# Chunk 0 of a sketched attention by halves of its tokens, with the remaining keys and one sketch load moved

## The chip, the cores and the metric

The kernel runs on one core of a Trainium2 chip. Its time is the device time of one execution in microseconds (us); smaller is better. The engines are PE (TensorE, with PEld for its weight loads), DVE (VectorE), ACT (ScalarE), POOL (GpSimd) and SP (SyncE, which here only issues DMAs). Each engine works through its own instructions in the order of the program text: the kernel ties every instruction to the one before it on its engine.

## The reference

Attention with sketched features, whose result goes into a two-layer perceptron with an exact gelu:

```python
batch, n_heads, seq, head_dim = (4, 4, 1088, 32)   # r = 8
def phi(x):
    a = np.einsum('rd,bhsd->bhsr', S1, x)
    b = np.einsum('rd,bhsd->bhsr', S2, x)
    return np.einsum('bhsi,bhsj->bhsij', a, b).reshape(*x.shape[:-1], r * r)
q_p, k_p = (phi(q), phi(k))
kv = np.einsum('bhsf,bhsd->bhfd', k_p, v)
z = np.sum(k_p, axis=2)
num = np.einsum('bhsf,bhfd->bhsd', q_p, kv)
den = np.einsum('bhsf,bhf->bhs', q_p, z)[..., None] + 1e-06
x = (num / den)              # to (4352, 128): tokens by heads * head_dim
h = x @ w_in                 # 128 -> 2048
g = 0.5 * h * (1.0 + erf(h * inv_sqrt2))
out = g @ w_out              # 2048 -> 128
```

S1, S2, w_in and w_out come as float64; q, k and v as float32.

## The kernel before, in words

**Tokens.** Each of the four batches has 1088 tokens: 1024 in two chunks of 512, and 64 that remain. So there are eight chunks (n = 0 to 7) and one last chunk of the remaining tokens of all batches. For each chunk the 2048 hidden features are 16 tiles `fi` of 128: `hidden(n, fi)` is one product of 128x128 by 128x512 on PE (two passes of 0.43 us each in fp32) into a bank `h_ps`, of which there are two, and a gelu on ACT from it, which frees the bank. `project` and `two_products` multiply the gelus by w_out.

**Prologue.** Before this stream runs, batch 0 needs its attention. The names:
- `sketches` turns the sketch S (S1 above S2) on PE (L319). S itself arrives as float64 words in `raw_SR` (L177) and is rounded to float32 by `Rounding` into `SR_heads`.
- `key_turn` transposes keys on PE (L333), `key_features` multiplies them by the sketches (L375) and forms the features `k_p` on DVE or POOL.
- `key_turn_rem` and `key_features_rem` do so for the 64 remaining keys of batches 0 and 2 (L333, L399, then L404 and L405).
- `kv_first` and `kv_first_rem` sum features by values into `kv_bank` (L432, L438), with the sums z as extra columns; the result is copied to `kz[0]` by ACT (L794).
- `query_turn(n)` transposes queries: chunk 1 on PE (L333, then a copy `qT` by ACT), the others on DVE. `expand_products(n)` (L497) expands them on PE into two double banks `w_ps`; `expand_copy` copies one factor out on ACT to `A_sb` (L504), `expand_multiply` makes `q_pT` on DVE (L510).
- `attend_by_token(n)`, for chunks 0 and 1, multiplies `q_pT` by `kz` (L562, tokens on the partitions), adds 1e-6 to the denominators (L567), inverts them (L568) and multiplies (L570) into `x_tok`; `turn_x` transposes that on PE (L578) and copies it to `xT` on ACT and DVE (L581), which `hidden` reads.

**Weights.** Every piece of w_in and w_out arrives as float64 words and is rounded by `Rounding` in steps: `low_words` and `exponents` on ACT (L267, L279), `fields`, `mantissas` and `signs` on DVE (L271, L273, L287, L292), and `product` on DVE or POOL (L297). The first two pieces of each have 256 columns.

**Loads.** Nearly all are issued by SP in the order of the text. `load_w_out(i, gated=True)` first lets POOL write one element of the landing tile (L168), so that SP can't issue the load before POOL has come there; everything SP issues later stands behind it.

**Order.** Until step 4 the order is written out by hand; then `steps` gives the order of `hidden(n, fi)`, first features 0 to 3 of chunk 0, then those of chunk 1, and so on, with slots between them. `keep_busy` issues a product of noughts whose result nobody reads. Lines whose order the change touches:

```python
    query_turn(1, lambda **a: late.append(a))
    act.copy(out=kz[0], in_=kv_bank[:, :128])
    ...
    banks = [hidden_bank(), hidden_bank()]
    attend_by_token(0, banks)
    expand_products(1)
    w_in[1].mantissas()
    expand_copy(1, 0)
    turn_x(0, [hidden_bank(), hidden_bank()])
    keep_busy(1, out_bank())
```

Of the kernel before, what the change touches and what calls it, by code (L numbers as in the profile page):

```python
# [16 lines left out]
def kernel(  # L17
# [49 lines left out]
    def work_banks():  # L67

        return wps.tile([128, 2, CW], FP, name="w_ps")
# [93 lines left out]
    def load_w_out(i, gated=False):  # L163
        src, e = words(moe_w_out)
        to = landing(w_out_sb[i], e == 2)
        if gated:

            pool.memset(to[0:1, 0:1], 0)  # L168
        sp.dma_start(
            out=to.rearrange("p (fo d) -> p fo d", d=d_model * e),  # L170
            in_=src[slice(*pieces[i]), :].rearrange("(fo fi) d -> fi fo d", fi=128))

    S_dst = landing(SR, S1.dtype != FP)

    for i, s in enumerate((S1, S2)):
        s, e = words(s)
        act.dma_start(out=S_dst[i * R:(i + 1) * R, :], in_=s)  # L177
    nc.scalar.preload_act_table_set("gelu_and_others")
    for r in range(2):
        load_main(sp, "k", 0, slice(r, H, 2))  # L180
# [217 lines left out]
    def key_features_rem(pair, ps, by_pool=False):  # L398
        pe.matmul(ps[:, 384:448], lhsT=kT["rem"][:, :128], rhs=S12.rearrange("p h r -> p (h r)"), start=True, stop=True)  # L399
        k_p_rem[pair] = big.tile([128, H, R, R], FP, name=f"k_p_rem{pair}")  # L400
        ab = ps[:, 384:448].rearrange("p (h r) -> p h r", r=2 * R)
        both = att.tile([128, H, 2 * R], FP, name="a_rem")
        if by_pool:
            act.copy(out=both, in_=ab)  # L404
            pool.tensor_mul(**spread(k_p_rem[pair], both[:, :, 0:R], both[:, :, R:2 * R]))  # L405
            return
        a = both[:, :, 0:R]
        act.copy(out=a, in_=ab[:, :, 0:R])
        dve.tensor_mul(**spread(k_p_rem[pair], a, ab[:, :, R:2 * R]))
# [16 lines left out]
    def kv_first(ps, r, tokens=range(J)):  # L426

        for i in tokens:

            ch, t, one = i // 4, i // 2 % 2, i % 2  # L430
            for c in range(NP):
                pe.matmul(ps[c * F:(c + 1) * F, r * 2 * D:(r + 1) * 2 * D], lhsT=flat(k_p[0, r][:, t, c * 4 + ch * 2 + one]),  # L432
                          rhs=v_aug[r][:, c, i, :], start=(r == 0 and i == 0), stop=False, skip_group_check=True)
# [68 lines left out]
    def expand_copy(n, i):  # L502
        A[i] = att.tile([128, 2, CW // 2], FP, name="A_sb")
        act.copy(out=A[i][:, :, :width[n] // 2], in_=B_of[n][i][:, :, :width[n] // 2])  # L504
# [44 lines left out]

    x_tok = {}  # L550

    def attend_by_token(n, banks, meanwhile=lambda: None):

        x_tok[n] = att.tile([128, JC, H, D], FP, name="x_tok", bufs=1)
        den = att.tile([128, NP, JC * 2], FP, name="den_tok")
        for i in range(JC):
            for r in range(2):
                for half in range(2):
                    for c in range(NP):
                        rows, at, tok = slice(c * F, (c + 1) * F), (i * 2 + r) * C, i * 128 + half * 64  # L560
                        v_at = kz_cols(0, 2 * c + r)[0]
                        pe.matmul(banks[c][half * 64:(half + 1) * 64, at:at + C], lhsT=qp[n][rows, r, tok:tok + 64],  # L562
                                  rhs=kz[0][rows, v_at:v_at + C], start=True, stop=True)
        meanwhile()
        nd = [banks[c][:, :JC * 2 * C].rearrange("p (g c) -> p g c", c=C) for c in range(NP)]
        for c in range(NP):
            dve.tensor_scalar(out=den[:, c], in0=nd[c][:, :, D], scalar1=1e-6, scalar2=None, op0=AX.add)  # L567
        dve.reciprocal(out=den, in_=den)  # L568
        for c in range(NP):
            dve.tensor_mul(out=x_tok[n][:, :, 2 * c:2 * c + 2], in0=nd[c][:, :, 0:D].rearrange("p (j r) d -> p j r d", r=2),  # L570
                           in1=den[:, c].rearrange("p (j r) -> p j r", r=2)[:, :, :, None].broadcast_to([128, JC, 2, D]))

    def turn_x(n, banks):

        xT[n] = att.tile([128, CW], FP, name="xT", bufs=3)
        for i, ps in enumerate(banks):
            for j in range(2):
                pe.transpose(ps[:, j * 128:(j + 1) * 128], in_=x_tok[n][:, 2 * i + j].rearrange("p h d -> p (h d)"),  # L578
                             identity=ident)
        for i, (ps, copy) in enumerate(zip(banks, (by_act, by_dve))):  # L580
            copy(out=xT[n][:, i * 256:(i + 1) * 256], in_=ps[:, :256])  # L581


    g_of, o_of = {}, {}
# [1 line left out]
    def w_tile(w, fi):  # L586
        i = max(i for i, (c0, c1) in enumerate(pieces) if c0 <= fi * 128)
        at = fi * 128 - CUTS[i]
        return w[i][:, at:at + 128]

    def hidden(n, fi, by_halves=False):
        W = width[n]
        ps = hidden_bank()
        w = w_tile(w_in_sb, fi)
        for rows in (slice(0, 64), slice(64, 128)) if by_halves else (slice(0, 128),):
            pe.matmul(ps[rows, :W], lhsT=w[:, rows], rhs=xT[n][:, :W], start=True, stop=True)  # L596
        if n < NCH and fi < USUAL:
            g_of[n, fi] = mlp.tile([128, CW], FP, name="g", bufs=4)
        else:
            if fi % NB == 0:  # L600
                blocks[n, fi // NB] = block(FP)
            g_of[n, fi] = blocks[n, fi // NB][:, fi % NB]
        act.activation(out=g_of[n, fi][:, :W], in_=ps[:, :W], func=ACT.Gelu)  # L603

# [172 lines left out]
    for i in range(2):  # L777
        query_features(0, i)
    kv_bank = out_bank()
    kv_first(kv_bank, 0)  # L780
    key_turn_rem(0, banks[1], by_act)
    kv_first(kv_bank, 1, range(J // 2))
    key_features_rem(0, banks[1], by_pool=True)
    load_w_out(0, gated=True)
    kv_first(kv_bank, 1, range(J // 2, J))
    kv_first_rem(kv_bank)
    w_in = [Rounding(w) for w in w_in_sb[:2]]
    w_out = [Rounding(w_out_sb[0], beside=w_in[0])]
    w_in[0].low_words()
    w_in[0].fields()  # L790
    w_in[0].exponents()
    late = []
    query_turn(1, lambda **a: late.append(a))
    act.copy(out=kz[0], in_=kv_bank[:, :128])  # L794
    w_in[1].low_words()
    by_act(**late[0])
    w_in[0].mantissas()
    w_in[0].signs()
    w_in[0].product(pool)
    w_in[1].fields()  # L800
    load_rest()
    w_out.append(Rounding(w_out_sb[1], beside=w_in[1]))
    w_in[1].exponents()
    banks = [hidden_bank(), hidden_bank()]
    attend_by_token(0, banks)
    expand_products(1)
    w_in[1].mantissas()
    expand_copy(1, 0)
    turn_x(0, [hidden_bank(), hidden_bank()])
    keep_busy(1, out_bank())  # L810
    w_in[1].signs()
    w_in[1].product(pool)
    expand_copy(1, 1)
    for i in range(2):
        expand_multiply(1, i)
    w_out[0].fields()


# [129 lines left out]
    for t in range(len(steps) + LAG):  # L948
        if t < 4:

            hidden(0, t)
            if t == 1:
                w_out[0].exponents()
                w_out[0].low_words()
                w_out[0].finish()
                w_out[1].fields()
            if t == 2:
                w_out[1].low_words()
            if t == 3:
                attend_by_token(1, halves(work_banks()), lambda: (w_out[1].mantissas(by_pool=True),  # L960
                                                                  w_out[1].exponents()))
                w_out[1].signs()
                w_out[1].product()
                for u in range(4):
                    for f, *a in products[u]:
                        f(*a)
            continue
        if t == 4:
            turn_x(1, [work_bank(), work_bank()])
            for f, *a in products[t]:  # L970
                f(*a)
        for n in drains[t]:
            drain(n)
        if t < len(steps):
            n, fi = steps[t]
            hidden(n, fi, by_halves=t >= 18 and (n < NMAIN or fi < 5))
        if t < len(steps) and steps[t][0] < NMAIN and steps[t][1] % NB == NB - 1:
            n, b = steps[t][0], steps[t][1] // NB
            if b >= first_block(n):
                token_sums(n, b)  # L980
        for f in slots[t]:
            f()
        for n in done[t]:
            store(n)
        if t != 4:
            for f, *a in products[t]:
                f(*a)
# [41 lines left out]
```

## Time and profile before

| | |
|---|---|
| median of 4 runs | 272.45 us (271.41 to 273.43) |
| the profiled execution | 273.18 us |
| its span, first to last instruction | 271.4 us |
| PE busy | 265.9 us, 98% |
| DVE, ACT, POOL busy | 153.2, 136.7, 170.0 us |
| first hidden product of chunk 0 starts | 18.10 us |
| numerators of chunk 1 start (L562) | 21.86 us |
| first hidden product of chunk 1 starts | 26.34 us |

In the profile's timelines the columns are the start, the duration, the engine, the line of the kernel, the operation, what it writes and reads, and in brackets how long the engine was idle before it and what ended that. The chain of waits runs back from the last instruction to what released each one. Starts are counted from the span's first instruction. A PE duration holds its pipeline, so consecutive rows overlap.

### The profile page before, as it was taken

To read this page: it belongs to the slowest core of one execution; us is meant where nothing else is said; L and a number is where in the kernel's file an instruction comes from. 1 tells how busy PE (TensorE), PEld (TensorE's weight loads), DVE (VectorE), ACT (ScalarE), POOL (GpSimd) and SP (SyncE) were. 2 spreads that over 40 slices of the span, in tenths; PEclk is the share of its full clock that TensorE was granted. 3 is DMA by queue.
4 is the path that set the end of the run, shared out by engine and by line. 5 is a ranking of instruction groups with operands and counts; after the bars stand their busy time and mean duration, and the time that the engine had idled before them with its cause. 6 is when DMAs were issued, how large, how long until landed. Compare 5 with 4: busy or idle time off the path is not lost.

```text
span 271.4 us, 6237 instructions
## 1 busy us (share of the span) xinstructions
PE 265.9 (98%) x2557; PEld 138.9 (51%) x2557; DVE 153.2 (56%) x242; ACT 136.7 (50%) x272; POOL 170.0 (63%) x178
## 2 busy tenths in 40 slices
PE   8999999999999999999999999999999999999994
PEld 6755444454454545444445445444443544455794
DVE  5676678623793699569314897288017901760140
ACT  4455767466645633483347533573357343734431
POOL 3422005899998488368865797568866886777400
PEclk9999999999999999999999999999999999999999
DMA  6469363525101100110200000100200020011020
GB/s 197 130 226 341 65 168 68 169 61 170 30 0 24 19 0 2 17 24 1 41 1 2 0 2 8 33 2 0 39 2 0 2 40 2 0 21 21 1 42 20
DMA packets 37869, 13.52 MB, mean 50 GB/s; under 512 B 28240, under 2 KB 37200, under 8 KB 37840
## 3 DMA queue, kind: packets, MB, share of 16 engines
q1 hardware_dynamic: 37648, 13.05, 18.7%
q8 instruction: 20, 0.33, 0.5%
q10 hardware_dynamic: 192, 0.07, 0.1%
q14 instruction: 9, 0.07, 0.1%
HBM read 10.88 MB, written 2.23 MB: 48 GB/s over the span
## 4 chain that ended last, share of the span: by engine, by line
PE 96%; DVE 1%; DMA 1%; issue 0%; POOL 0%; ACTq 0%; ACT 0%; DVEq 0%
PE h_ps L596 44%; PE o_ps L673 32%; PE o_ps L724 5%; PE w_ps L497 3%; PE w_ps L721 3%; PE w_ps L537 2%; PE w_ps L444 2%; PE w_ps L375 1%; DMA raw_SR<-in_S_dram 1%; PE o_ps L432 1%; PE h_ps L562 0%; PE w_ps L562 0%; PE h_ps L333 0%; PE o_ps L375 0%; PE h_ps L375 0%; PE o_ps L333 0%
## 5 line engine op out<-in xcount | busy, mean ns | idle before, releaser
L596 PE MATMUL h_ps<-xT,w_in 128*64 128x512 f32 (+3 forms) x518 | 140.8, 577 | 0.2 <-DVE xT L581 0.2
L603 ACT ACTIVATE block<-h_ps 128x512 f32<-128x512 f32 (+1 forms) x128 | 72.8, 571 | 101.5 <-PE h_ps L596 98.4
L673 PE MATMUL o_ps<-block,w_out 128*64 128x256 f32 x224 | 57.9, 381 | 0.0
L596 PEld LDWEIGHTS h_ps<-xT,w_in 128*64 128x64 f32 (+1 forms) x518 | 42.1, 143 | 29.6 <-issue 9.6
L638 POOL TENSOR_TENSOR bits_low<-block 128x512 f32<-128x512 f32 x28 | 36.4, 1301 | 27.8 <-ACT block L603 27.6
L673 PEld LDWEIGHTS o_ps<-block,w_out 128*64 128x64 f32 x224 | 30.0, 137 | 36.9 <-issue 27.7
L639 POOL TENSOR_TENSOR bits_a<-block 128x512 f32<-128x512 f32 x28 | 36.1, 1288 | 15.9 <-ACT block L603 15.6
L641 POOL TENSOR_TENSOR bits_m<-block,bits_e 128x512 f32<-128x512 f32 x28 | 36.3, 1297 | 2.2
L640 POOL TENSOR_TENSOR bits_e<-bits_a,block 128x512 f32<-128x512 f32 x28 | 36.2, 1293 | 2.2
L544 DVE RECIPROCAL den<-den 128x512 f32<-128x512 f32 (+1 forms) x7 | 21.9, 3122 | 14.0 <-ACT den L543 14.0
L673 PE MATMUL o_ps<-bits_a,small 128*64 128x256 f32 x112 | 29.0, 382 | 0.0
L673 PE MATMUL o_ps<-bits_m,w_out 128*64 128x256 f32 x112 | 28.8, 380 | 0.0
L673 PE MATMUL o_ps<-bits_low,small 128*64 128x256 f32 x112 | 28.7, 379 | 0.0
L673 PE MATMUL o_ps<-block,small 128*64 128x256 f32 x112 | 28.7, 379 | 0.0
L510 DVE TENSOR_TENSOR q_pT<-A_sb,w_ps 128x512 f32<-128x512 f32 x16 | 10.4, 683 | 31.3 <-ACT A_sb L504 31.3
L689 DVE TENSOR_TENSOR sums<-o_ps,sums 64x512 f32<-64x512 f32 x8 | 5.5, 683 | 35.9 <-ACT sums L686 20.4
L673 PEld LDWEIGHTS o_ps<-block,small 128*64 128x64 f32 x112 | 15.3, 137 | 18.0 <-issue 12.8
L548 DVE TENSOR_TENSOR xT<-w_ps,den 32x512 f32<-32x512 f32 (+1 forms) x28 | 18.2, 649 | 1.4 <-DVE den L544 0.5
L673 PE MATMUL o_ps<-bits_e,small 128*64 128x256 f32 x112 | 16.8, 379 | 0.0
L724 PE MATMUL o_ps<-g,w_out 128*128 128x512 f32 x32 | 16.4, 600 | 0.1
L543 ACT ACTIVATE den<-w_ps 32x512 f32<-32x512 f32 (+1 forms) x28 | 15.6, 558 | 1.3 <-PE w_ps L537 1.0
L673 PEld LDWEIGHTS o_ps<-bits_low,small 128*64 128x64 f32 x112 | 15.3, 137 | 0.0
(160 smaller groups left out, 316.8 us busy)
## 6 DMA issues: line engine op xcount, KB each, us to landing
block<-in_moe_w_in_dram SPq DMA_DIRECT2D x3, 512.0 KB, 5.8
block<-in_moe_w_out_dram SPq DMA_DIRECT2D x3, 512.0 KB, 9.1
k<-in_k_dram SPq DMA_DIRECT2D x48, 32.0 KB, 1.9
v<-in_v_dram SPq DMA_DIRECT2D x3, 512.0 KB, 4.0
q<-in_q_dram SPq DMA_DIRECT2D x24, 64.0 KB, 3.0
out_dram<-oT SPq DMA_DIRECT2D x24, 64.0 KB, 2.2
k<-in_k_dram SPq DMA_DIRECT2D x2, 256.0 KB, 2.8
q<-in_q_dram SPq DMA_DIRECT2D x2, 256.0 KB, 4.2
```

Source lines behind the costliest of these rows:

```text
L510: dve.tensor_mul(out=qp[n].rearrange("f r (g x) -> f g r x", g=G)[:, 2 * i:2 * i + 2], in0=a, in1=b)
L543: act.activation(out=den[h * D:(h + 1) * D, :W], in_=banks[h // 2][at:at + D, :W], func=ACT.Copy, bias=1e-6)
L544: dve.reciprocal(out=den[:, :W], in_=den[:, :W])
L548: dve.tensor_mul(out=xT[n][rows, :W], in0=banks[h // 2][at:at + D, :W], in1=den[rows, :W])
L596: pe.matmul(ps[rows, :W], lhsT=w[:, rows], rhs=xT[n][:, :W], start=True, stop=True)
L603: act.activation(out=g_of[n, fi][:, :W], in_=ps[:, :W], func=ACT.Gelu)
L638: pool.tensor_sub(out=s[3], in0=a11, in1=a21)
L639: pool.tensor_add(out=s[1], in0=a21, in1=a22)
L640: pool.tensor_sub(out=s[2], in0=s[1], in1=a11)
L641: pool.tensor_sub(out=s[4], in0=a12, in1=s[2])
L673: pe.matmul(acc[n][bank][half * 64:(half + 1) * 64, col:col + HW], lhsT=fixed, rhs=moving, start=opens and e == 0 and name in "4715", stop ...
L724: pe.matmul(o_of[n], lhsT=w_tile(w_out_sb, fi), rhs=g, start=first, stop=final)
```

## The change

- The second sketch S2 is loaded by SP, ahead of the keys; S1 stays on ACT's queue.
- The remaining keys are transposed after four of the eight token groups of the first `kv_first`; their features are multiplied out after the first two groups of the second, and formed by ACT and DVE instead of ACT and POOL.
- `attend_by_token` is split into `numerators_by_token` and `divide`, `turn_x` into `turn_half`; chunk 0 goes through them in two halves of 256 tokens, the first half through two `h_ps` banks and the second through a double `w_ps` bank. `x_tok` is two tiles.
- Features 0 and 1 of chunk 0 are multiplied in two halves of columns by `first_hidden`; `hidden` then only takes the gelu of them.
- `query_turn(1)` now follows the numerators, `expand_products(1)` stands between the two halves of `first_hidden`, and both copies and multiplications of chunk 1's queries follow.
- The gated load of w_out[0] and `load_rest` follow w_in[0]'s product on POOL; w_in[1]'s product moves from POOL to DVE. The `keep_busy(1)` before chunk 0's products is gone.

```diff
-    for i, s in enumerate((S1, S2)):
+    for i, (s, queue) in enumerate(((S1, act), (S2, sp))):
         s, e = words(s)
-        act.dma_start(out=S_dst[i * R:(i + 1) * R, :], in_=s)
+        queue.dma_start(out=S_dst[i * R:(i + 1) * R, :], in_=s)
...
+    def divide(n, banks, tokens, by_head_pair):
+
+        g = len(tokens) * 2
+        den = att.tile([128, NP, JC * 2], FP, name="den_tok")[:, :, :g]
+        parts = [slice(c, c + 1) for c in range(NP)] if by_head_pair else [slice(0, NP)]
+        nd = [(banks[c.start][:, None] if by_head_pair else banks)[:, :, :g * C].rearrange("p b (g c) -> p b g c", c=C)
+              for c in parts]
+        for c, x in zip(parts, nd):
+            dve.tensor_scalar(out=den[:, c], in0=x[:, :, :, D], scalar1=1e-6, scalar2=None, op0=AX.add)
         dve.reciprocal(out=den, in_=den)
...
+    def turn_half(n, i, ps, copy):
+        if i == 0:
+            xT[n] = att.tile([128, CW], FP, name="xT", bufs=3)
+        for j in range(2):
+            pe.transpose(ps[:, j * 128:(j + 1) * 128], in_=x_tok[n, i][:, j].rearrange("p h d -> p (h d)"), identity=ident)
+        copy(out=xT[n][:, i * 256:(i + 1) * 256], in_=ps[:, :256])
...
+    def first_hidden(half, fis):
+
+        for fi in fis:
+            if half == 0:
+                first_banks[fi] = hidden_bank()
+            cols = slice(half * 256, (half + 1) * 256)
+            pe.matmul(first_banks[fi][:, cols], lhsT=w_tile(w_in_sb, fi), rhs=xT[0][:, cols], start=True, stop=True)
...
-    kv_first(kv_bank, 0)
+    kv_first(kv_bank, 0, range(4))
     key_turn_rem(0, banks[1], by_act)
-    kv_first(kv_bank, 1, range(J // 2))
-    key_features_rem(0, banks[1], by_pool=True)
-    load_w_out(0, gated=True)
-    kv_first(kv_bank, 1, range(J // 2, J))
+    kv_first(kv_bank, 0, range(4, J))
+    kv_first(kv_bank, 1, range(2))
+    key_features_rem(0, banks[1])
+    kv_first(kv_bank, 1, range(2, J))
     kv_first_rem(kv_bank)
     w_in = [Rounding(w) for w in w_in_sb[:2]]
...
+    act.copy(out=kz[0], in_=kv_bank[:, :128])
     w_in[0].exponents()
...
     w_in[0].product(pool)
+    load_w_out(0, gated=True)
+    load_rest()
+    w_out = [Rounding(w, beside=b) for w, b in zip(w_out_sb[:2], w_in)]
+    first = [hidden_bank(), hidden_bank()]
+    second = work_banks()
+    numerators_by_token(0, first, range(2))
+    numerators_by_token(0, halves(second), range(2, JC))
+    query_turn(1)
+    divide(0, first, range(2), by_head_pair=True)
+    divide(0, second, range(2, JC), by_head_pair=False)
     w_in[1].fields()
...
+    turn_half(0, 0, out_bank(), by_act)
+    first_hidden(0, range(2))
+    w_in[1].low_words()
     w_in[1].exponents()
...
+    turn_half(0, 1, out_bank(), by_dve)
+    w_in[1].mantissas()
+    w_in[1].signs()
+    w_in[1].product()
     expand_products(1)
...
+    first_hidden(1, range(2))
     for i in range(2):
-        expand_multiply(1, i)
+        query_features(1, i)
     w_out[0].fields()
```

For chunk 1 (step 3) `attend_by_token` is replaced by `numerators_by_token`, the two rounding steps that stood inside it, and `divide`; `turn_x` by two calls of `turn_half`.

More of the change, by code (lines that the diff above doesn't have):

```diff
@@ L550, with numerators_by_token @@
     x_tok = {}
[L552 to L556, printed above, removed]
+    def numerators_by_token(n, banks, tokens):
+        for at, i in enumerate(tokens):
             for r in range(2):
@@ L559, in attend_by_token @@
                     for c in range(NP):
-                        rows, at, tok = slice(c * F, (c + 1) * F), (i * 2 + r) * C, i * 128 + half * 64
+                        rows, col, tok = slice(c * F, (c + 1) * F), (at * 2 + r) * C, i * 128 + half * 64
                         v_at = kz_cols(0, 2 * c + r)[0]
-                        pe.matmul(banks[c][half * 64:(half + 1) * 64, at:at + C], lhsT=qp[n][rows, r, tok:tok + 64],
+                        pe.matmul(banks[c][half * 64:(half + 1) * 64, col:col + C], lhsT=qp[n][rows, r, tok:tok + 64],
@@ L563, in attend_by_token @@
                                   rhs=kz[0][rows, v_at:v_at + C], start=True, stop=True)
[L564 to L567, printed above, removed]
-        dve.reciprocal(out=den, in_=den)
-        for c in range(NP):
-            dve.tensor_mul(out=x_tok[n][:, :, 2 * c:2 * c + 2], in0=nd[c][:, :, 0:D].rearrange("p (j r) d -> p j r d", r=2),
-                           in1=den[:, c].rearrange("p (j r) -> p j r", r=2)[:, :, :, None].broadcast_to([128, JC, 2, D]))
@@ L573, in turn_x, with x_half @@
[L573 to L581, printed above, removed]
+    def x_half(n, i):
+        x_tok[n, i] = att.tile([128, 2, H, D], FP, name=f"x_tok{i}", bufs=1)
+        return x_tok[n, i]
@@ new lines, in divide @@
+    def divide(n, banks, tokens, by_head_pair):
[6 more added lines that the diff above has]
+            dve.tensor_scalar(out=den[:, c], in0=x[:, :, :, D], scalar1=1e-6, scalar2=None, op0=AX.add)
+        dve.reciprocal(out=den, in_=den)
+        for i in range(len(tokens) // 2):
+            to = x_half(n, tokens[0] // 2 + i).rearrange("p j (c r) d -> p c j r d", c=NP)
+            for c, x in zip(parts, nd):
+                for b in range(c.stop - c.start):
+                    dve.tensor_mul(out=to[:, c.start + b], in0=x[:, b, i * 4:i * 4 + 4, 0:D].rearrange("p (j r) d -> p j r d", r=2),
+                                   in1=den[:, c.start + b, i * 4:i * 4 + 4].rearrange("p (j r) -> p j r", r=2)[:, :, :, None]
+                                   .broadcast_to([128, 2, 2, D]))
@@ L589, in w_tile @@
         return w[i][:, at:at + 128]
+    first_banks, begun = {}, [(0, 0), (0, 1)]
     def hidden(n, fi, by_halves=False):
         W = width[n]
-        ps = hidden_bank()
+        ps = first_banks.pop(fi) if fi in first_banks else hidden_bank()
         w = w_tile(w_in_sb, fi)
         for rows in (slice(0, 64), slice(64, 128)) if by_halves else (slice(0, 128),):
-            pe.matmul(ps[rows, :W], lhsT=w[:, rows], rhs=xT[n][:, :W], start=True, stop=True)
+            if (n, fi) not in begun:
+                pe.matmul(ps[rows, :W], lhsT=w[:, rows], rhs=xT[n][:, :W], start=True, stop=True)
         if n < NCH and fi < USUAL:
@@ L779 @@
     kv_bank = out_bank()
-    kv_first(kv_bank, 0)
+    kv_first(kv_bank, 0, range(4))
     key_turn_rem(0, banks[1], by_act)
-    kv_first(kv_bank, 1, range(J // 2))
-    key_features_rem(0, banks[1], by_pool=True)
-    load_w_out(0, gated=True)
-    kv_first(kv_bank, 1, range(J // 2, J))
+    kv_first(kv_bank, 0, range(4, J))
+    kv_first(kv_bank, 1, range(2))
+    key_features_rem(0, banks[1])
+    kv_first(kv_bank, 1, range(2, J))
     kv_first_rem(kv_bank)
     w_in = [Rounding(w) for w in w_in_sb[:2]]
-    w_out = [Rounding(w_out_sb[0], beside=w_in[0])]
     w_in[0].low_words()
     w_in[0].fields()
+    act.copy(out=kz[0], in_=kv_bank[:, :128])
     w_in[0].exponents()
[L792 to L796, printed above, removed]
     w_in[0].mantissas()
@@ L799 @@
     w_in[0].product(pool)
+    load_w_out(0, gated=True)
[8 more added lines that the diff above has]
+    divide(0, second, range(2, JC), by_head_pair=False)
     w_in[1].fields()
-    load_rest()
-    w_out.append(Rounding(w_out_sb[1], beside=w_in[1]))
+    turn_half(0, 0, out_bank(), by_act)
+    first_hidden(0, range(2))
+    w_in[1].low_words()
     w_in[1].exponents()
-    banks = [hidden_bank(), hidden_bank()]
-    attend_by_token(0, banks)
+    turn_half(0, 1, out_bank(), by_dve)
+    w_in[1].mantissas()
+    w_in[1].signs()
+    w_in[1].product()
     expand_products(1)
[L807 to L813, printed above, removed]
+    first_hidden(1, range(2))
     for i in range(2):
-        expand_multiply(1, i)
+        query_features(1, i)
     w_out[0].fields()
@@ L959 @@
             if t == 3:
-                attend_by_token(1, halves(work_banks()), lambda: (w_out[1].mantissas(by_pool=True),
-                                                                  w_out[1].exponents()))
+                banks = work_banks()
+                numerators_by_token(1, halves(banks), range(JC))
+                w_out[1].mantissas(by_pool=True)
+                w_out[1].exponents()
+                divide(1, banks, range(JC), by_head_pair=False)
                 w_out[1].signs()
@@ L968 @@
         if t == 4:
-            turn_x(1, [work_bank(), work_bank()])
+            for i, copy in enumerate((by_act, by_dve)):
+                turn_half(1, i, work_bank(), copy)
             for f, *a in products[t]:
```

## The prediction
> **What bounds the kernel now.** I read the page first, then the chain that ended last, then the timelines of the first 26 us engine by engine, because the diff changes nothing later. Page, parts 1 and 2:
>
> ```profile
> PE 265.9 (98%) x2557; PEld 138.9 (51%) x2557; DVE 153.2 (56%) x242; ACT 136.7 (50%) x272; POOL 170.0 (63%) x178
> PE   8999999999999999999999999999999999999994
> DMA  6469363525101100110200000100200020011020
> ```
>
> PE (TensorE) is full but for the first and last slices. All it does must be done in any order, so the change can only win or lose PE idle time before the steady stream starts. The chain, restricted to the first 32 us (start, length, what):
>
> ```profile
> 1.38 2.15 DMA raw_SR<-in_S_dram
> ...
> 4.79 0.28 PE w_ps L319
> 5.07 1.04 PE h_ps L333 x4
> ...
> 7.98 1.94 PE w_ps L497 x32
> 9.92 1.08 PE o_ps L432 x32
> ...
> 12.28 0.22 ACT a_rem L404
> 12.50 0.07 issue
> 12.57 0.62 POOL k_p_rem L405
> ...
> 16.86 0.64 PE h_ps L578 x4
> ...
> 17.53 0.44 DVE xT L581
> 17.96 0.14 issue
> 18.10 3.83 PE h_ps L596 x8
> 21.93 1.07 PE w_ps L562 x64
> ```
>
> From 4.79 on PE runs back to back except in three places: the remaining keys (12.86 to 13.25), x (16.42 to 16.86, and about 0.6 around the keep-busy matmul until 18.10), and 0.39 inside the eight hidden passes (3.83 for 8 x 0.43). ACT's (ScalarE's) timeline shows the order that matters below:
>
> ```profile
> 16.50 0.59 ACT L504 COPY A_sb<-w_ps 128x512 f32<-128x512 f32 x1 [1.18 <-PE w_ps L497]
> 17.31 0.37 ACT L581 COPY xT<-h_ps 128x256 f32<-128x256 f32 x1 [0.23 <-PE h_ps L578]
> 17.58 0.59 ACT L504 COPY A_sb<-w_ps 128x512 f32<-128x512 f32 x1
> 19.23 0.60 ACT L603 ACTIVATE g<-h_ps 128x512 f32<-128x512 f32 x1 [1.06 <-PE h_ps L596]
> ```
>
> Both copies of chunk 1's expanded queries lie in ACT's idle time ahead of the first gelu. Hidden pass 3 needs the bank that this gelu frees (19.83), and starts at 19.95.
>
> [...] at 17.58 the second copy stands behind xT though its data were there by 16.5. [...] L497 x32 takes 1.94 us at 7.98 and 1.12 at 15.28. [...] the issues here take 0.29 to 0.60 us.
>
> **The change, part by part** (times of the profiled execution).
>
> 1. *Second sketch on SP.* ACT's two issues took 0.60 and 0.29; SP's key issues 0.45 each, the first at 0.73. The sketch now goes first, so keys, q, v and the later loads on SP start 0.3 to 0.6 later, 0.45 taken. The first keys landed as PE started on them (3.61, after 2.85 us), so PE starts at 4.06. In return the sketch lands earlier than 3.53; but PE waited only 0.13 for SR_heads (transposes to 4.66, L319 at 4.79), so no more than that is won. L319 thus comes 0.3 later, and all PE work behind it. Until about 9.9 PE runs at half clock; if that moment stays put, half of the delay is made up. I take 0.25; from both sides -0.13 (keys not delayed) and +0.5.
>
> 2. *Remaining keys.* (The times from here leave out part 1's 0.25.) The transpose moves 0.54 forward, to 10.46 on PE; ACT copies it at 11.03, free of A_sb only then (before 11.30). L399 follows at 11.56 when PE reaches it, ACT's smaller copy ends at 12.16, and DVE's multiply of 128x256 (like L297, 0.43) replaces POOL's 0.62 and ends at 12.6. PE ends its kv matmuls at 12.84 as before; the wait of 0.39 is gone. kv ends at 13.29. Late next is kz: ACT copies it (0.27) and PE goes on at 13.73, since query_turn(1), which filled this hole, now stands behind the numerators. Stall 0.44 for 0.39: no gain from this pair alone, but kz is earlier by 0.4.
>
> 3. *Numerators and x by halves.* 0.57 per half (1.14 for 64 instructions): PE ends the first at 14.30, the second at 14.87, query_turn at 15.45. DVE: signs of w_in[0] wait for exponents, which now stand behind kz on ACT, and end at 14.54. Then two adds 0.24, reciprocal 0.25, two multiplies of 128x128 [...], and two gaps of 0.03: x half 0 at 15.5, half 1 (one add) at 16.4. PE waits from 15.45 to 15.63 (0.14 from DVE to PE, as at 17.96), transposes to 15.93. ACT copies qT first (15.5 to 16.08), then xT half 0 until 16.4; the first two products' first halves start on PE at 16.52: stall 0.59. They take 4 x 0.215, to 17.38.
>
> 4. *Behind them.* Transposes of half 1 (0.29), expand_products(1) (17.67 to 18.75), second halves (0.86, to 19.6; xT half 1, copied by DVE, is ready at 18.2 and hidden by the expansion). Now ACT: the two A_sb copies can't start before 18.85, when the expansion is done, and stand ahead of the first gelu: 18.85 to 19.95. Gelu 0 runs 19.93 to 20.53, where it ran 19.23 to 19.83. The third hidden pass starts at 20.65: stall 1.04 (before 0.39 in the eight passes). Four passes of 0.43: to 22.35, against 21.93.
>
> Check by idle time from 12.85 on: before, 9.08 us hold 7.33 of work and 1.75 idle, keep-busy counted as idle; after 7.26 and 0.44 + 0.18 + 0.59 + 1.04 = 2.25. Loss 0.42.
>
> 5. *Then.* w_out[0]'s rounding waits for the same gelus on ACT and ends at about 23.05, PE asks at 23.4 plus: hidden. For chunk 1 DVE has one add less but four multiplies of 128x128 in place of two of 128x256 [...], so w_out[1]'s product ends at 25.7, PE resumes at 25.84, before 25.41. The loss stays 0.43.
>
> 6. *Loads.* w_out[0]'s load was issued at 13.25; its gate now stands on POOL behind w_in[0]'s product (to 15.3), so SP issues it at about 15.6, and w_in[2] at 17 instead of 15.25. On SP everything behind, down to keys and values of batches 1 to 3, is 1.8 to 2.1 later. Cover: w_out[0] landed in 3.2, so by 19, and DVE asks at 20.7. w_in[2] and its neighbours land in 5.8 to 9.1, asked for from 26 on. v_rem released POOL at 40.36, and POOL then idled 3.37 before its next product. Cost nothing; without the cover, up to 1 us.
>
> Removed: one keep-busy matmul (0.6, in idle time). POOL gives w_in[1]'s product to DVE (0.43, before 19.4, asked for at 20.65).
>
> Sum: 0.25 + 0.42 = +0.67. The execution profiled took 273.18 for a span of 271.4, so 1.78 around it; it would become 272.1 and 273.85. It lies 0.73 above the median of the runs, so from the median 272.45 I get 273.1.
>
> **Rivals.**
> *A, a little faster: 272.2.* The copies of A_sb start when their own bank is done, at about 18.3, the stall of 1.04 shrinks to 0.5, and keys come no later (-0.13): 0.42 - 0.54 - 0.13 = -0.25. For it: the copies read the two banks apart. Against: at 16.50 and 9.96 they started only when all of L497 had ended.
> *B, clearly slower: 276.2.* [...] The price: at the start PE worked from 3.61 to 9.9 before full clock came, 6.3 us at half rate, that is 3.15 lost, on top of 273.1. For it: the keep-busy matmul is gone and the longest stall nearly triples. Against: [...] before, 1.75 idle did not trip it. [...]
> *C, loads late: 274.1.* POOL or DVE wait for part 6's loads after all, 1 us. Against: the slack above.
> *D, the change does less than it says:* ACT's order eats the halves' gain; that is the forecast itself.
>
> **Numbers.** Forecast 0.62, A 0.23, B 0.07, C 0.08. The measurement of this kernel tells about 1% (2.7 us) from no change: four runs span 271.41 to 273.43. The forecast's own range, from -0.13 and +0.5 in part 1 and half a microsecond for the stalls and for the spread of medians, is 272.0 to 274.4; with A and C taken in, each with a quarter to half a microsecond of its own, 271.7 to 274.6, which leaves out B and the outer ends. Faster by over 1% needs 2.7 us where all idle of 12.85 to 25 is 1.8: 0.02. Slower: B: 0.07. Same: 0.91.
>
> **What would show it.** First key transposes on PE at about 4.05, not 3.61; kv_first_rem directly after the kv matmuls; both A_sb copies ahead of the first gelu, which starts near 20.2 (part 1 included); a stall near 1 us before the third hidden pass; the second chunk's first hidden pass near 27.0, before 26.4; the granted clock full from about 10 us. Wrong if that pass comes before 26.4, if L497's second expansion or the passes take twice their time (B), or if a wait on a DMA stands between 20 and 50 us on DVE or POOL (C).

## The result

The changed kernel takes 272.92 us (median of 43 runs, 272.02 to 275.54), the kernel before 271.78 us beside it (64 runs, 271.25 to 274.70): a ratio of 1.0044, 95% interval 1.0027 to 1.0061. Forecast were 273.1 and a loss of 0.67; the loss is 1.14.

The runs of each kernel fall into groups, after the moment at which TensorE's clock becomes full (9.9 us in the trace of a late run of the kernel before, 4.8 in that of an early one; experiment 3): of the kernel before, 43 of the 64 runs lie at 271.2 to 272.3 and 21 at 273.1 to 274.7; of the changed kernel, 26 of 43 at 272.0 to 273.1 and 17 at 274.0 to 275.5. Below, those under the gap are called early runs, the others late ones. Their medians here are 271.61 and 272.57, so 0.96 of the 1.14 lies among the early runs, and the remaining 0.18 is there because more of the changed kernel's runs are late (17 of 43 against 21 of 64, a difference that chance can make).

The profile of before that the prediction read (273.18 us) is of a late run, that of the changed kernel (272.53 us, span 270.7) of an early one. So the kernel before was profiled once more (`e1_before`: 271.37 us, span 269.6), and it is this trace that the changed kernel is compared with.

The page of the changed kernel, parts 1 and 2:

```profile
PE 263.8 (97%) x2559; PEld 138.1 (51%) x2559; DVE 155.3 (57%) x249; ACT 136.4 (50%) x272; POOL 167.5 (62%) x176
PE   8989999999999999999999999999999999999994
```

PE is nearly as full as before (97% for 98%); only the third slice (13.5 to 20.3 us) has lost a tenth. The chain of the changed kernel that ended last, to 26 us (start, length, what):

```profile
8.17 0.69 PE o_ps L432 x16
...
11.17 0.44 PE o_ps L438 x8
...
14.78 1.10 PE h_ps L623 x4
...
18.87 1.98 PE h_ps L608 x4
20.85 1.07 PE w_ps L560 x64
...
25.47 1.72 PE h_ps L608 x4
```

and the same of the kernel before, from `e1_before`:

```profile
8.05 1.13 PE o_ps L432 x32
...
11.43 0.45 PE o_ps L438 x8
...
16.28 3.83 PE h_ps L596 x8
20.11 1.07 PE w_ps L562 x64
...
24.70 1.72 PE h_ps L596 x4
```

Read both at four points ("kv" below stands for the sums of features by values). The sums of features by values start at 8.05 before and 8.17 after, and end (L438) at 11.88 and 11.61: this stretch became 0.39 shorter. From there to chunk 1's numerators (L562, now L560) it is 8.23 before and 9.24 after: 1.01 longer. From these to chunk 1's first hidden product, 4.59 and 4.62. From that product to the end of the span, 244.9 and 245.2. So 0.12 - 0.39 + 1.01 + 0.03 + 0.3 = 1.07, of 1.1 between the spans. This is one trace of each kernel; what holds over many runs is measured below. Part of the lengthening stands on ACT's timeline of the changed kernel:

```profile
17.24 1.07 ACT L504 COPY A_sb<-w_ps 128x512 f32<-128x512 f32 x2 [1.88 <-PE w_ps L497]
18.20 1.10 ACT L615 ACTIVATE g<-h_ps 128x512 f32<-128x512 f32 x2
```

ACT idles for 1.88 us, then has both copies of the expanded queries to make before the first gelu, and PE waits 0.66 us for that gelu before its third hidden product (the prediction's "third hidden pass").

### The profile page after: what moved, and what is told of

It reads as the page before. It is cut to its first block, busy times and chain, and to the rows that moved or that the text cites. A ratio compares the mean times of both kernels' runs of the same rounds, so it can differ in the third digit from the quotient of the medians.

```text
span 270.7 us, 6249 instructions
## 1 busy us (share of the span) xinstructions
PE 263.8 (97%) x2559; PEld 138.1 (51%) x2559; DVE 155.3 (57%) x249; ACT 136.4 (50%) x272; POOL 167.5 (62%) x176
## 4 chain that ended last, share of the span: by engine, by line
PE 91%; POOL 3%; DMA 1%; ACT 1%; issue 1%; SPq 0%; DVE 0%; POOLq 0%
PE h_ps L608 41%; PE o_ps L693 31%; PE o_ps L744 5%; PE w_ps L497 3%; PE w_ps L741 3%; PE w_ps L537 2%; DMA q<-in_q_dram 1%; PE w_ps L444 1%; PE w_ps L375 1%; POOL bits_r L418 1%; PE o_ps L432 1%; PE w_ps L560 1%; POOL bits_r L421 1%; POOL bits_e L660 0%; POOL bits_a L659 0%
## 5 line engine op out<-in xcount | busy, mean ns | idle before, releaser
L608 PE MATMUL h_ps<-xT,w_in 128*64 128x512 f32 (+3 forms) x514 | 138.9, 577 | 0.7 <-ACT g L615 0.7
L608 PEld LDWEIGHTS h_ps<-xT,w_in 128*64 128x64 f32 (+1 forms) x514 | 41.4, 142 | 28.9 <-issue 8.6
L709 DVE TENSOR_TENSOR sums<-o_ps,sums 64x512 f32<-64x512 f32 x8 | 5.5, 683 | 35.7 <-ACT sums L706 20.2
L744 PE MATMUL o_ps<-g,w_out 128*128 128x512 f32 x32 | 16.4, 599 | 0.1
```

The source lines that it names most:

```text
L744: pe.matmul(o_of[n], lhsT=w_tile(w_out_sb, fi), rhs=g, start=first, stop=final)
```

## The experiments

### 1. Each part put back or done alone

`e1_before` is the kernel before, unchanged:

> The kernel before, unchanged, for a second trace. The two traces differ in when PE runs its 128x128 transposes at 0.145 us instead of 0.26 us: from 4.1 us on in the profile after, from about 9.9 us in the profile before. If that moment is a matter of chance and not of the change, this run can show either; with the early one its span is about 269.8 (271.55 of device time), and chunk 1's first hidden pass starts near 24.7, against 25.47 in the profile after. If the change moved that moment, this run shows 9.9 again.

It took 271.37 us and shows an early clock, as used above.

`e2_sketch` is the kernel before with the second sketch on SP:

```diff
-    for i, s in enumerate((S1, S2)):
+    for i, (s, queue) in enumerate(((S1, act), (S2, sp))):
...
-        act.dma_start(
+        queue.dma_start(
```

> The kernel before with the second sketch on SP ahead of the keys, nothing else. Theory of the prediction: keys come 0.45 later, +0.25 us in the end (ratio 1.0009). Rival 1: where PE is at full clock from about 4 us, the queries' landing (6.12 in the profile after, 6.15 before, though issued 0.42 later) sets the pace and the later keys cost nothing: ratio 1.000. Rival 2: the sketch is what costs most of the +1.2 us: ratio 1.003 or more.

Measured: 273.55 (22 runs, 271.63 to 274.63), ratio 1.0033 (1.0006 to 1.0061). Of the 22 runs 9 are early, with a median of 271.76, against 271.49 for the 32 early ones of 43 of the kernel before beside it: +0.27 among the early runs. The other 13 lie at 273.4 to 274.6. By the ratio alone the second rival would hold, but most of the ratio is the share of late runs, 13 of 22 against 11 of 43 beside it. Its profiled execution is a late one, like that of the kernel before in the prediction. The chain of `e2_sketch`:

```profile
0.73 0.40 SPq L177
...
1.19 2.85 DMA k<-in_k_dram
...
8.39 1.93 PE w_ps L497 x32
...
18.50 3.83 PE h_ps L596 x8
22.34 1.07 PE w_ps L562 x64
```

SP is busy for 0.40 us with a sketch of 2 KB, the keys start at 1.19, and from L497 on the rows stand 0.40 or 0.41 after their likes in the prediction's chain (7.98, 18.10, 21.93). Nothing of it was made up at the change of clock, which itself came at 10.2 us in place of 9.9.

`e5_act` is the changed kernel with both sketches on ACT:

```diff
-    for i, (s, queue) in enumerate(((S1, act), (S2, sp))):
+    for i, s in enumerate((S1, S2)):
```

> The changed kernel with both sketches on ACT's queue again, as before. Theory: the sketch ahead of the keys costs twice: the queries land 0.2 to 0.6 us later (about 0.35 us on PE's path), and PE has nothing from 3.67 to 4.06 (keep-busy over, keys not there), so that full clock comes at about 4 us in fewer runs and only at about 10 us in more of them. Undone, the early runs fall from 272.5 to about 272.1, and the late ones are about 3 in 10, as for the kernel before, instead of 4 in 10: median near 272.1. Rival: the sketch cost under 0.1 us and the share of late runs is chance: early runs stay at 272.4 or more.

Measured: 272.39 (22 runs), ratio 1.0018 (0.9999 to 1.0038); 18 of 22 runs early, median 272.31, against 271.62 beside it: +0.69. That is 0.2 above what was expected, and less of the loss goes than the theory had it. The changed kernel's own +0.96 thus holds about 0.27 of the sketch, as in `e2_sketch` from the other side. What is left is the rest of the change.

`e7_keys` is the kernel before with the new order of the remaining keys alone:

```diff
-    kv_first(kv_bank, 0)
+    kv_first(kv_bank, 0, range(4))
     key_turn_rem(0, banks[1], by_act)
-    kv_first(kv_bank, 1, range(J // 2))
-    key_features_rem(0, banks[1], by_pool=True)
+    kv_first(kv_bank, 0, range(4, J))
+    kv_first(kv_bank, 1, range(2))
+    key_features_rem(0, banks[1])
     load_w_out(0, gated=True)
-    kv_first(kv_bank, 1, range(J // 2, J))
+    kv_first(kv_bank, 1, range(2, J))
```

> The kernel before with only the new order of the remaining keys: turned amid the first kv, features by ACT and DVE; the gate of w_out[0]'s load follows them as before and so comes some 2 us earlier on POOL. Theory: the wait of 0.39 ahead of kv_first_rem goes, and here query_turn(1) still stands behind it and fills the copy of kz: 0.3 to 0.4 us faster than before (ratio 0.9987, early runs at 271.1). Rival: kz comes no earlier for the numerators because PE is full with query_turn until then, or DVE's multiply delays w_in[0]'s rounding: no change.

Measured: 271.46 (14 runs), ratio 0.9995 (0.9973 to 1.0017); 9 of 14 runs are early, with a median of 271.36 against 271.62 beside it: 0.26 less, where 0.3 to 0.4 was expected. The interval of the ratio holds no change; experiment 3 repeats the step against a kernel that differs in this alone.

`e4_loads` is the changed kernel with the loads that the prediction's part 6 speaks of issued early again, `e8_halves` is that with both sketches on ACT too, so that parts 2 to 5 remain (and the moves that the prediction held to cost nothing):

```diff
     key_features_rem(0, banks[1])
+    load_w_out(0, gated=True)
+    load_rest()
     kv_first(kv_bank, 1, range(2, J))
...
     w_in[0].product(pool)
-    load_w_out(0, gated=True)
-    load_rest()
```

> The changed kernel with the gated load of w_out[0] and all the rest issued right after the remaining keys' features, some 4 us earlier. Theory: the later loads cost 0.3 us near 50 to 60 us (v_rem releases POOL at 42.85 instead of 40.36[...], and PE waits for bits_e at 59.6); early loads give that back: 0.3 us on the changed kernel (ratio to before 1.0033). Rival 1: that wait comes from elsewhere, nothing won. Rival 2: early weights collide with nothing now but with the keys and values of batch 1 later, or with the last prologue loads, and it is slower.

> The changed kernel with both sketches on ACT and the loads issued early: what is left of the change is the remaining keys and chunk 0 by halves. Theory: sketch 0.35 and loads 0.3 undone, the halves' loss of about 1.0 and the keys' gain of 0.39 stay: early runs near 271.9 to 272.1, 0.4 to 0.6 above before (271.45), chunk 1's first hidden pass 0.6 us later than in the early trace of before (24.70). Rival: the halves cost nothing themselves and all came from the sketch and the loads: early runs at 271.5 or less.

Measured: `e4_loads` 272.59, ratio 1.0039 (1.0013 to 1.0065), early median 272.35 against 271.49, +0.86 where the changed kernel had +0.96; `e8_halves` 272.39, ratio 1.0012 (0.9991 to 1.0033), early median 272.34 against 271.62, +0.72 where `e5_act`, with the late loads, had +0.69. So the late loads cost between nothing and 0.1 us; what `e8_halves` loses, 0.1 above its expected range, is the cost of the remaining change. Yet the profiled execution of the changed kernel lost a further 0.3 late: from chunk 1's first hidden product to the end it took 245.2, in each of the thirteen other traces 244.9. From its timelines of DVE and of POOL, and then its chain:

```profile
44.15 1.75 DVE L271 TENSOR_SCALAR bits_e<-block 128x512 uint32<-128x512 uint32 x1
```

```profile
47.97 1.27 POOL L297 TENSOR_TENSOR w_out<-bits_m,bits_e 128x512 f32<-128x512 f32 x1 [1.77 <-DVE bits_e L292]
```

```profile
49.84 1.27 POOL bits_r L418
...
59.62 0.65 PE o_ps L693 x4
```

The values of the remaining tokens (v_rem) hold POOL until 42.85 (40.36 in the prediction's trace), and its next product then comes 0.13 us later, counted from chunk 1's first hidden product, than in all other traces. The delay that counts begins beside it, on DVE: its step at 44.15 takes 1.75 us, in the thirteen other traces 0.39 at this place. POOL waits for DVE, comes 0.6 late to L418, and PE stands still at 59.62 until POOL has delivered. `e3_gelu`, `e5_act` and `e6_busy` have the late loads too and show neither. So this wait was seen once, with late loads; that POOL's 0.13 set off the long step of DVE is possible and not shown.

### 2. What holds the first products back

Parts 3 and 4 cost 1.01 us. The theory is the order on ACT. `e3_gelu` is the changed kernel with each of the first two gelus ahead of one copy of the expanded queries:

```diff
     for i in range(2):
+        hidden(0, i)
         query_features(1, i)
...
-            hidden(0, t)
+            if t >= 2:
+                hidden(0, t)
```

> The changed kernel with gelu 0 ahead of the first A_sb copy and gelu 1 ahead of the second. Theory: the stall ahead of the third hidden pass (0.66 in the profile after) is ACT's order; it goes, gelu 0 starts near 17.6 instead of 18.2 and the kernel wins 0.4 to 0.55 us on the changed one (ratio to before 1.0025 instead of 1.0044). Rival: the copies then come later, q_pT is late for chunk 1's numerators or w_out[0]'s rounding for the first L744, and nothing or under 0.2 us is won.

Measured: 276.38 (6 runs, 273.95 to 276.72), ratio 1.0133 (1.0081 to 1.0184). Only one of the six runs, the profiled one with 273.95, lies anywhere near the early ones, 1.4 above those of the changed kernel; the other five are above 276, so the ratio mixes groups. In its trace the third hidden product does start earlier, 18.89 with L497 at 7.43, where the changed kernel has 18.87 with L497 at 7.00: 0.41 earlier relative to L497. Then a new wait stands in PE's list, of 1.4 us, longer than the one that went (0.7 for the gelu, now 0.3):

```profile
PE o_ps L744 <- DVE w_out L297: 1.4, 1, 1.4
```

The second copy now follows the second gelu, DVE's multiplication waits for it, and the rounding of w_out[0] stands behind that multiplication on DVE. Chunk 1's first hidden product comes at 27.29 (25.47 in the changed kernel): the 1.4 us, and 0.4 from the start.

`f4_order` asks whether that rounding was all that stood in the way. It has the gelus as in `e3_gelu`, sketches and loads as in `e8_halves`, and w_out[0]'s first steps moved into idle time before the expansion:

```diff
     w_in[1].fields()
+    w_out[0].fields()
     turn_half(0, 0, out_bank(), by_act)
...
     w_in[1].exponents()
+    w_out[0].exponents()
+    w_out[0].low_words()
```

> The changed kernel with both sketches on ACT and the early loads; w_out[0]'s fields, exponents and low words rounded before the expansion of chunk 1's queries, in DVE's and ACT's idle time, and each of the first two gelus ahead of one copy of the expanded queries (copy and gelu in turn). Theory 'the loss of the changed part is ACT's two copies ahead of the first gelu, and undoing that failed only since the rounding of w_out[0] stood behind': no wait of TensorE for w_out[0], the third hidden pass 0.5 to 0.6 earlier against the end of kv, chunk 1's numerators 8.6 to 8.8 us after the end of kv, time 271.7 to 271.9. Rival 'another wait takes its place' (the second copy, one gelu later, makes chunk 1's numerators wait): 9.2 and 272.3 or more.

Measured: 272.74 (14 runs, 272.51 to 275.89), ratio 1.0033 (0.9999 to 1.0067), so not the 271.7 to 271.9 of the theory. Chunk 1's numerators come 8.9 us after the end of kv (12.23 to 21.12), 0.4 sooner than in `e8_halves`, though short of the 8.6 to 8.8 expected. But chunk 1's first hidden product comes 14.42 after kv, where `e8_halves` has 13.93. Its chain shows why:

```profile
20.52 0.69 DVE q_pT L510
...
24.98 0.44 DVE w_out L297
...
25.55 1.10 PE o_ps L744 x2
```

The second copy (20.01), a gelu later, moves all that follows on DVE, and PE waits 0.73 for the rounding of w_out[1] in place of w_out[0]. Theory and rival both have a part: ACT's order makes most of the stall (0.26 of the 0.66 us is left), and undoing it hands the time to DVE's queue.

The other question was why four passes (two products of two passes each) took 1.98 after the stall and not 4 x 0.43. `f3_fill` is `e8_halves` with two products of noughts in the stall:

```diff
     first_hidden(1, range(2))
+    keep_busy(2, out_bank())
```

> The changed kernel with both sketches on ACT and the early loads, as in the last call, and two products of noughts put into TensorE's stall of 0.66 us ahead of the third hidden pass. Theory 'restart': four passes that took 1.98 us after the stall take 1.72, and chunk 1's numerators come 8.98 us after the end of kv in place of 9.27; time 0.25 below the 272.34 of the same kernel without them. Rival 'the passes are only drawn long by the trace, or the stall is paid anyway': still 9.27 or more, time 272.3 or above.

Measured: 272.37 (22 runs), ratio 1.0023 (0.9998 to 1.0048), early median 272.25 against 271.51, +0.74 where `e8_halves` has +0.72. PE's timeline of `e8_halves`, then that of `f3_fill`:

```profile
19.04 1.98 PE L608 MATMUL h_ps<-xT,w_in 128*128 128x512 f32 x4 [0.66 <-ACT g L615]
...
22.08 1.98 PE L744 MATMUL o_ps<-g,w_out 128*128 128x512 f32 x4
```

```profile
19.05 1.94 PE L608 MATMUL h_ps<-xT,w_in 128*128 128x512 f32 x4
```

The rival holds: with PE at work right up to them the four passes start at the same moment and take 1.94 in place of 1.98, and the numerators come 9.24 after kv against 9.28. Nor does a stall go ahead of L744, whose four passes take 1.98 as well. So the quarter of a microsecond is no restart. In the traces each pass lasts 0.59 and the next starts 0.43 after it; the first after other work lasts 0.65 to 0.70, with 0.49 to 0.53 to the next. The last pass of a group thus ends 0.16 beyond its 0.43, and a first one adds up to 0.10: together the 0.26. It comes with a group of passes that follows other work, after a stall or not; in `f3_fill`'s chain 0.16 of it is only counted for the products of noughts. Why a first pass is longer stays open.

### 3. When the full clock comes

In the two traces of the unchanged kernel the first PE rows tell the groups apart. First the one that the prediction read, a late run, then `e1_before`, an early one:

```profile
3.61 1.09 PE L333 MATMUL h_ps<-ident,k 128*128 128x128 f32 x4
...
5.00 1.11 PE L333 MATMUL h_ps<-ident,k 128*128 128x128 f32 x4
```

```profile
3.59 1.09 PE L333 MATMUL h_ps<-ident,k 128*128 128x128 f32 x4
...
5.01 0.66 PE L333 MATMUL h_ps<-ident,k 128*128 128x128 f32 x4
```

Same program, same waits, yet from 5.0 on the same transposes take 0.66 instead of 1.11. The traces' own record of the granted clock has its first entry, full clock, at 9.9 us in the first and at 4.8 in the second. In the fourteen traces of this case it lies at 9.9, 10.2 and 12.3 in the three of late runs, and between 3.7 and 6.8 in the others. With the sketch on SP there is a new hole ahead of these rows: PE's start-up products of noughts end at 3.67 and the keys come at 4.09 in the changed kernel. So one product more was put there, in the changed kernel (`e6_busy`), in the kernel before (`f2_busy`), and in the kernel before with the new order of the keys (`f1_best`):

```diff
     keep_busy(3, bank)
+    keep_busy(1, bank, 128)
```

> The changed kernel with one more keep-busy product of 128 columns (two passes, 0.43 us at half clock) behind the three, so that PE is busy from 0.77 until the keys land near 4.06. Theory: the hole in PE's work is what makes early full clock rarer; filled, late runs become 3 in 10 or fewer (4 in 10 without), the early ones stay at 272.3 to 272.6 because the queries' landing sets their pace. Rival: the hole plays no part; the share of late runs stays at 4 in 10 or more.

> The kernel before with one more product of noughts at the start and nothing else. Theory of the full clock: the 30 in 100 runs at 273.2 to 274.8 vanish and the rest stay at 271.5 plus at most 0.2 for the extra product, so the median hardly moves (ratio 0.998 to 1.001). Rival: their share stays.

> The kernel before with the new order of the remaining keys and with one more product of noughts at the start, to bridge TensorE's wait for the sketch or the keys. Theory 'the time of full clock decides between groups of runs': no run above 273.1 us, median 0.2 under that of the before runs with an early full clock (271.4 against 271.6), so a ratio of 0.997 to 0.999. Rival 'the groups have another cause': runs at 273.2 to 274.8 stay as frequent as in the kernel before (about 30 in 100). Full clock from 4 to 6.5 us in the trace.

| kernel | median | ratio to before, 95% interval | late runs | median of the early runs, and of before beside it |
|---|---|---|---|---|
| `e6_busy` | 272.53 | 1.0014 (0.9997 to 1.0030) | 1 of 22 | 272.52, 271.62 |
| `f2_busy` | 271.67 | 0.9968 (0.9949 to 0.9987) | 1 of 22 | 271.66, 271.51 |
| `f1_best` | 271.40 | 0.9970 (0.9954 to 0.9986) | 0 of 22 | 271.40, 271.51 |

The medians hide most of this, since they lie among the early runs anyway; the ratio does not. Over all comparisons the kernel before had 83 late runs of 241, kernels with the sketch on SP and no product more (the changed one, `e2_sketch`, `e4_loads`) 38 of 87, those with the product more 2 of 66. The product takes nearly all late runs away; in `f2_busy` it costs the early ones about 0.15, which is within their scatter. That the empty stretch at 3.7 to 4.1 makes late runs more frequent agrees with 38 of 87, but this difference is not large enough to be called shown. Nor is closing that stretch what helps: the kernel before has none (its keys are taken up at 3.59 or 3.61, before the products of noughts end), and there the product works as well. What it shifts is the moment: full clock comes at 6.4, 6.6 and 6.8 us in the three traces with it. Why is open.

`f1_best` and `f2_busy` differ in the order of the keys alone, and both traces are of early runs. `f2_busy`, then `f1_best`:

```profile
8.77 1.15 PE o_ps L432 x32
...
11.48 0.63 POOL k_p_rem L405
12.16 0.45 PE o_ps L438 x8
```

```profile
8.89 0.69 PE o_ps L432 x16
...
11.90 0.43 PE o_ps L438 x8
```

From the start of L432 to the end of L438 it is 3.84 and 3.44: POOL's `k_p_rem` has left the chain, and the early medians differ by 0.26, as by 0.26 in `e7_keys`. `f1_best` is faster than both kernels: 0.9970 of the kernel before (0.9954 to 0.9986), where the changed kernel has 1.0044. Most of this is the late runs that it lacks; among early runs it is 0.11 below the kernel before, which is within their scatter.

## Why the prediction was right, and where it was off

- **The number, and luck.** 273.1 lies 0.2 from the 272.92 measured, but by luck in part: it was reckoned from 272.45, the median of four runs of which two were late, and that stands 0.67 above the 271.78 of 64 runs. The loss itself, 0.67, was 0.3 short of the 0.96 among early runs and 0.47 short of the 1.14.
- **Part 1, the sketch, +0.25.** Right in size: +0.27 (`e2_sketch`) and 0.27 (`e5_act`). Two reasons given for it were not. "Half of the delay is made up" at the change of clock: the late trace of `e2_sketch` is 0.40 behind at the end of the prologue as at its start. And where the full clock is early, the path need not go through the keys: in the changed kernel's trace q lands at 6.12 and L497 waits for DVE's `qT` made from it. Over the traces q lands at 6.12 to 6.55 (middle 6.39) with the sketch on SP and at 5.79 to 6.81 (middle 6.09) without, which agrees with the 0.27 but does not prove the path.
- **Part 2, the remaining keys.** Shown as worked out: the sums follow each other without a wait, 0.39 less. "No gain from this pair alone" held for the changed order, in which `kz` is waited for (PE idles 0.35); where `query_turn(1)` still covers that wait, 0.26 is won (`e7_keys`, and `f1_best` against `f2_busy`).
- **Parts 3 and 4, loss 0.42 with part 2.** Nearly every step came in its place: less the 1.68 by which kv ends earlier in the changed kernel's trace (13.29 to 11.61), the prediction has the first products at 14.84 (14.78 measured), the first gelu at 18.25 (18.20), the third product at 18.97 (18.87) and chunk 1's numerators at 20.67 (20.85). The lengths reckoned with for DVE's multiplies of 128x128 were an estimate that no trace of before shows; in the changed kernel's trace (L581) two take 0.49 together and chunk 1's four 0.89, where two of 128x256 took 0.76 (L570). The term that was mis-sized is the passes: twice "4 x 0.215" and once "four passes of 0.43" make 3.44, and PE needed 1.10, 0.95 and 1.98 for them, 4.03. The prediction had met this surplus and read it as idle time: of the 3.83 for eight passes before, it took 0.39 for a stall, but PE waited for the gelu only 0.09 there, and the rest is what groups of passes last beyond their 0.43 apiece (experiment 2). In return the stall ahead of the third product was 0.66 and not 1.04, and kz cost 0.1 less; with smaller differences 0.2 of the 0.6 is left. Loss of parts 2 to 4 in the traces 1.01 - 0.39 = 0.62; in the times 0.69 (`e5_act`) and 0.72 (`e8_halves`).
- **Part 5.** Hidden, as costed: 4.62 for 4.59 between chunk 1's numerators and its first hidden product.
- **Part 6, nothing.** Nothing to 0.1 in the times. But the cover was thinner than the prediction's 3.37 of idle POOL: in the changed kernel's profiled run v_rem came 0.13 later than POOL could have used it. The wait at 59.62 in that run, 0.3 us where rival C has 1, starts from a long step on DVE; whether the loads are behind it is not shown.
- **Rival A** failed where it was said to: ACT's copies wait 1.88 us for the expansion and start only at its end (17.24). **Rival B**, a loss of full clock behind PE's stalls, failed: L497's second expansion takes 1.16 in the chain, where the prediction's trace has 1.94 ahead of full clock and 1.12 (its row at 15.28) behind it. What the clock did do was elsewhere and not foreseen: its start, not its fall, moves whole runs by about 2 us, and the prediction took one late trace ("full clock from about 10 us") for the kernel's habit; the changed kernel's trace has it from 4.2. Ahead of full clock PE has half its later pace in the prediction's trace: passes of 128x256 on noughts (L755) start 0.43 apart from 1.33 on and 0.22 apart at 17.33. PE had there been at work almost without a break since 0.77, for 9.1 us, when full clock came.
- **The signs.** Keys on PE at 4.05 (4.09), sums without a wait and both copies ahead of the first gelu came as listed. Gelu near 20.2, chunk 1's first product near 27.0 and full clock at 10 did not (18.20, 25.47, 4.2), and "wrong if before 26.4" was met: the run traced was an early one, so these times tell nothing of the mechanism. Against the early trace of before the product comes 0.77 later (24.70 to 25.47). The sign for C, a wait on a DMA between 20 and 50 us, could not tell either, since POOL waits 14.55 us for v_rem in the trace of before too.
- **The sum.** 0.25 + 0.42 = 0.67 against 0.96 among the early runs: 0.2 for the passes, and 0.1 that is not placed, to which the late loads may belong. Another 0.18 of the median is the larger share of late runs, for which the prediction had no term.

That the moment of full clock varies the traces show: 4.8 and 9.9 us in two executions of the same kernel, 3.7 to 12.3 over all fourteen. The reason no run here shows.

## What to carry to other kernels

Split work to start an engine early only after reading the queue of the engine that takes over: here the first products started 1.5 us sooner (14.78 for 16.28) and the gelu that PE needed next then stood behind two copies on ACT; both ways tried round that moved the wait to DVE. And price a few passes by what such a group took in the trace, not by the pass alone: here the surplus was 0.6 us over twelve passes. Before comparing two profiles, check from the durations of the first matmuls (here four transposes in 0.66 us or in 1.09 to 1.11) that both reached full clock at about the same time. A small load set ahead of large ones on the same queue was not free here: 2 KB took SP 0.40 us to issue, PE's work behind the loads came 0.40 later in `e2_sketch`'s trace, and the early runs lost 0.27.

## What the runs showed of the hardware

- Late runs, 83 of 241 in the kernel before, were 2 of 66 in three kernels with one more start-up product of noughts, 0.43 us of PE time. Full clock came at 6.4 to 6.8 us in their traces.
- The page's row of the granted clock did not show this: it reads 9 in every slice of nine of these profiles, the three late ones among them, also where L333 takes 1.09 to 1.11 in place of 0.66. The durations do.
- Four passes of 128x512 last 1.98 us from their first start to their last end after a stall of 0.66 (L608), 1.98 without a stall (L744) and 1.94 behind products of noughts (`f3_fill`).
- One `bits_e` step of DVE (L271, 128x512) took 1.75 us at 44.15 in the changed kernel's trace, beside work on POOL, where the same step took 0.39 in all thirteen other traces. Why was not tried.
